# w1 of a decode MLP in one load of 28 KB to a partition, and the last rows of wo in the small slot

## The chip, the cores and the metric

The kernel runs on one core of a Trainium2 chip. The metric is device time in microseconds (us): 392.85 us for the kernel before, the median of 3 runs (392.83 to 392.96). All arithmetic is float32.

## The reference

One decode step (one token for each of B = 8 sequences) through an attention block over a sliding window of a cache and an MLP with a squared relu, both with adaptive layer norm. What is computed:

```python
W = min(4096, max(256, Sk // 4))                      # 2048 of 8192 cached positions
mod = (silu(c) @ w_mod).reshape(8, 6, 1, -1)          # sa, ca, ga, sb, cb, gb
h = layernorm(x) * (1 + ca) + sa
q = (h @ wq)                                          # 32 query heads, 8 kv heads, head size 128
scores = einsum("bhqd,bhkd->bhqk", q, k[:, :, Sk - W:]) * 128 ** -0.5
o = einsum("bhqk,bhkd->bhqd", softmax(scores), v[:, :, Sk - W:])
x = x + ga * (o.reshape(8, 1, 4096) @ wo)             # wo: 4096 x 512
h = layernorm(x) * (1 + cb) + sb
r = relu(h @ w1 + b1)                                 # w1: 512 x 1792
x = x + gb * ((r * r) @ w2 + b2)                      # w2: 1792 x 512
```

## The kernel before, in words

The keys and values of the window are 8 x 8 x 2048 x 128 numbers each and dominate what is read. For each of the 8 kv heads the kernel loads K in two pieces (4 sequences each) and V in two pieces, 4 MB to a piece: K 0 to K 15 and V 0 to V 15. A piece fills 32 KB of each of the 128 partitions.

SBUF has four **big slots** of 32 KB to a partition (one tile, `home`) and one **small slot** of 16 KB (tile `small`). Every large operand passes through one of them. The list `loads` (L186 to L193) names the loads in the order in which they are issued; `pump` (L196) issues from its head as long as the slot size that the next load needs has a free slot, and `done(key)` (L201), called where the last reader of an operand is written in the program, gives a slot back and pumps again. All these loads are issued by SyncE (SP) on one queue, except two gathers of wo rows by GpSimd. Each transfer signals one of eight completion semaphores, DMAHW0 to DMAHW7, which are used in turn: a load also waits until the transfer that used its semaphore before has landed.

The main loop (L586) runs over 38 steps. VectorE transposes K (L234), TensorE makes the scores (L405), a softmax follows (`soft_a` to `soft_g`), and five steps behind the scores come the products with V (L491, `weighted`). For each pair of heads `project_o(j)` (L538) multiplies the attention output with 1024 rows of wo (L544). Of the four pieces of wo rows, j = 0, 1, 2 pass through the small slot under the keys ("wo", j); the last one, j = 3, comes under the key ("tail", 0).

What comes at the end of the program:

- ("tail", 0) is a big slot that holds two things: the last wo rows in its first 16 KB and the first half of w1 (14 KB to a partition) behind them. Two loads fill it (L148 and L136).
- ("w1", 0) is the second half of w1, 14 KB to a partition, in the small slot (L136).
- ("w2", 0) is w2, 28 KB to a partition, in a big slot. It comes in four loads (L136) of 8, 4, 1 and 1 of its 14 row blocks.
- ACT issues five very small loads of b1 and b2 (L580).

After the last `project_o` the tail of the program is one chain. wo's result is added to x (L655, L656), the mean is taken over partitions with a matmul (L660), the normalized rows are turned (L241), and TensorE multiplies them with w1 (L688): for each of 4 row blocks kc, 4 matmuls, each of which is listed as two instructions. Between kc = 1 and kc = 2 stands the matmul of the variance (L683). `w1t[kc // 2]` says that kc = 0, 1 read the tail slot and kc = 2, 3 the small slot. Then b2 enters (L703), VectorE forms the squared relu (L241, L698 to L700), and TensorE multiplies with w2 (L707): 14 blocks f of 4 matmuls. `spin(n)` (L640, L643) puts n matmuls on the identity, whose result nobody reads, at three places of this tail. L715, L716 and a 64 KB store end the program.

Of the kernel before, what the change touches and what calls it, by code (L numbers as in the profile page):

```python
# [20 lines left out]
def tile_adaln_cached_attention_mlp(  # L21
# [16 lines left out]
    B, HKV, SK, DH = k_cache.shape  # L38
    D = wq.shape[0]
# [3 lines left out]
    F = w1.shape[1]  # L43
    NJ = 4 * W // P
    NQ = D // P
    FG = F // NQ
# [58 lines left out]
    big = NJ * DH  # L105
# [7 lines left out]
    held = {}  # L113

    def size_of(key):
        return "small" if key[0] in ("wo", "w1", "far") or key == ("mod", 1) else "big"

    def load(key):
        kind, i = key
        held[key] = free[size_of(key)].pop(0)  # L120
        if key == ("wq", 0):
            return
        t = slots[size_of(key)][held[key]]
        if kind in "KV":

            hk, c = divmod(i, 2)
            v = k_cache[4 * c : 4 * c + 4, hk] if kind == "K" else v_cache[c::2, hk]
            v = v[:, SK - W :, :].rearrange("u (p j) d -> p u (j d)", j=NJ)
            cuts = (0, big // 2, big) if key == ("V", 2 * HKV - 1) else (0, big)
            for x, y in zip(cuts, cuts[1:]):  # L130
                nc.sync.dma_start(t[:, x:y], v[..., x:y])
            return

        def rows(o, v):
            n = v.shape[1] * v.shape[2]
            nc.sync.dma_start(t[:, o : o + n].rearrange("p (a n) -> p a n", n=v.shape[2]), v)  # L136

        w1v = w1.rearrange("(p kc) n -> p kc n", p=P)

        def wo_rows(j):  # L140

            r = 2 * REP * DH
            if j < 2:
                v = wo[j * r : (j + 1) * r].rearrange("(b s) n -> b s n", s=32)[:, :28].rearrange("b (g i) n -> b g (i n)", i=7)
                nc.sync.dma_start(t[:, : 7 * D], v)
                return
            v = wo[j * r : (j + 1) * r, :].rearrange("(p i) n -> p (i n)", p=P)
            nc.sync.dma_start(t[:, : big // 2], v)  # L148

        if kind == "wo":  # L150
            wo_rows(i)
        elif kind == "far":

            nc.gpsimd.memset(t[:, : 4 * D], 0.0)  # L154
            nc.gpsimd.indirect_dma_start(
                out=t[:, : 4 * D],
                out_offset=None,
                in_=wo.rearrange("(a r) n -> a (r n)", r=4),
                in_offset=bass.IndirectOffsetOnAxis(ap=pieces[:, i : i + 1], axis=0),
                bounds_check=wo.shape[0] // 4 - 1,  # L160
                oob_is_err=False,
            )
        elif kind == "mod":

            v = w_mod.rearrange("(p kc) n -> p (kc n)", p=P)
            nc.sync.dma_start(t, v[:, big:] if i else v[:, :big])
        elif kind == "wq":

            o = base[held["wq", 0]]
            nc.sync.dma_start(home[:, o : o + 2 * big], wq.rearrange("(p k) n -> p (k n)", p=P))  # L170
        elif kind == "tail":
            wo_rows(HKV // 2 - 1)
            rows(big // 2, w1v[:, 0:2])
        elif kind == "w1":
            rows(0, w1v[:, 2:4])
        else:
            v = w2.rearrange("(p c) n -> p c n", p=P)
            for lo, hi in ((0, 8), (8, 12), (12, 13), (13, 14)):
                rows(D * lo, v[:, lo:hi])

    def slot(key, n, o=0):

        t = slots[size_of(key)][held[key]][:, o:]
        return t[:, : t.shape[1] // n * n].rearrange("p (a n) -> p a n", n=n)

    loads = [("mod", 0), ("mod", 1), ("wq", 0), ("wq", 1), ("K", 0), ("K", 1)]  # L186
    for n in range(2, 2 * HKV):
# [2 lines left out]
        if n in (4, 11, 14):  # L190
            loads.append(("wo", (4, 11, 14).index(n)))
        loads += [("K", n), ("V", n - 2)]
    loads += [("V", 2 * HKV - 2), ("V", 2 * HKV - 1), ("tail", 0), ("w1", 0), ("w2", 0)]  # L193
    at = [0]

    def pump():  # L196
        while at[0] < len(loads) and free[size_of(loads[at[0]])]:
            load(loads[at[0]])
            at[0] += 1

    def done(*keys):  # L201
        for k in keys:
            free[size_of(k)].append(held.pop(k))
        pump()
# [112 lines left out]
    for i, last in enumerate((16, 8)):  # L317
        at_ = 0
        while at_ < last:
            kc, m = divmod(16 * i + at_, 6)  # L320
# [25 lines left out]
    for kc in range(NQ):  # L346
        w = slot(("wq", kc // 2), 512)[:, kc % 2 * 8 : kc % 2 * 8 + 8]
# [190 lines left out]
    def project_o(j):  # L538

        last = j == HKV // 2 - 1  # L540
        key = ("tail", 0) if last else ("wo", j)
        w = slot(key, D)
        for i in range(8 if j > 1 else 7):
            nc.tensor.matmul(  # L544
                wo_ps[32 * (i % 4) : 32 * (i % 4) + 32, :],
                oT[:, i, :],
                w[:, i, :],
                start=(j == 0 and i < 4),
                stop=(last and i >= 4),
            )  # L550
        if j < 2:

            px = ps_m.tile([P, 512], F32, name="m_ps", tag="m_ps")
            for r in range(4):
                nc.tensor.matmul(px[:, 32 * r : 32 * r + 32], fsel[:, r], oT[:, 7, :], start=True, stop=True)
            px = px[:, :P].rearrange("p (r b) -> p r b", b=32)
            nc.scalar.copy(oX[:, :4], px)
        if not last:
            done(key)

    def far_rows(j):

# [23 lines left out]
    for s in range(N + PV_LAG + 1):  # L586
        g, i = divmod(s, C)
# [16 lines left out]
        if v > C and v % (2 * C) == 1 and v < N:  # L604
            project_o(v // C // 2 - 1)
# [26 lines left out]
        if ends:  # L632
            gather(v // C - 1)

    project_o(HKV // 2 - 1)


# [33 lines left out]
    ssb = work.tile([P, B], F32, name="ssb")  # L671
    nc.vector.tensor_scalar(ssb, sel[:, :B], ssq, None, op0=ALU.mult)

    w1t = [slot(("tail", 0), F, big // 2), slot(("w1", 0), F)]
    w2t = slot(("w2", 0), D)
    ph = ps_m.tile([P, 512], F32, name="m_ps", tag="m_ps")
    nc.tensor.matmul(ph[:, :FG], bsel.rearrange("p g b -> p (g b)"), b1_in, start=True, stop=False)
# [1 line left out]
    for kc in range(NQ):  # L679
        if kc == 2:  # L680

            pb = ps_m.tile([P, 512], F32, name="m_ps", tag="m_ps")
            nc.tensor.matmul(pb[:, :B], ones, ssb, start=True, stop=True)  # L683
            rstd = work.tile([P, B], F32, name="rstd_b")
            nc.scalar.activation(rstd, pb[:, :B], AF.Sqrt, bias=eps, scale=1.0 / D)
            nc.vector.reciprocal(rstd, rstd)
        for g in range(NQ):
            nc.tensor.matmul(  # L688
                ph[32 * g : 32 * g + 32, :FG],
                h2T[:, kc, :],  # L690
                w1t[kc // 2][:, kc % 2, g * FG : (g + 1) * FG],
                start=False,
                stop=(kc == NQ - 1),
            )
# [59 lines left out]
```

## Time and profile before

| what | value |
|---|---|
| timed runs, median of 3 | 392.85 us (392.83 to 392.96) |
| span of the profiled execution, first to last instruction | 390.9 us |
| timed median less that span | 1.95 us |
| PE busy | 260.2 us, 67% |
| DVE busy | 224.2 us, 57% |
| ACT busy | 46.7 us, 12% |
| DMA | 165.04 MB in 7157 packets, mean 422 GB/s |
| SyncE's queue (q1) | 164.17 MB in 6768 packets |

The span is what the profile sees of one execution; the timed runs hold what lies before the first and behind the last instruction as well. All times inside the program are in us from the start of the span. An engine's busy share is an average over the whole span; where it waits, and for what, is read from the chain of waits and from the timeline. PE is TensorE, DVE VectorE, ACT ScalarE, SPq the queue of SyncE.

### The profile page before, as it was taken

How to read it: one execution, taken by the hardware profiler on the slowest of the kernel's cores; microseconds unless marked ns; L12 is line 12 of the kernel's file. 1: busy time of each engine (PE TensorE's matmuls, PEld its weight loads, DVE VectorE, ACT ScalarE, POOL GpSimd, SP SyncE). 2: the span in 40 equal slices, each digit the busy share in tenths (PEclk: the TensorE clock that was granted, in tenths of full speed). 3: DMA queues.
4: the chain of work that ended last, by engine and by line, in shares of the span. 5: the costliest groups of instructions: out<-in, count | busy, mean ns of one | idle time of the engine just before them, and what ended most of it. 6: DMA issues, size and time to landing. Idle time of an engine off the chain costs nothing.

```text
span 390.9 us, 4829 instructions
## 1 busy us (share of the span) xinstructions
PE 260.2 (67%) x2066; PEld 81.8 (21%) x2066; DVE 224.2 (57%) x316; ACT 46.7 (12%) x91; POOL 10.2 (3%) x36
## 2 busy tenths in 40 slices
PE   0080958868337973798379737783788237996895
PEld 0030211112011321242113212321222011322433
DVE  1360099879057935775579457391789057855231
ACT  0120011221003100310031003100201003004010
POOL 4000000000000000030000000200000000000000
PEclk9997789999859996999599969989799859998999
DMA  8999999999999999999999999999999999999995
GB/s 330 431 436 423 434 443 436 438 426 403 441 429 429 431 433 433 431 438 419 431 424 433 431 443 423 428 433 428 433 428 419 443 436 428 425 433 420 416 433 224
DMA packets 7157, 165.04 MB, mean 422 GB/s; under 512 B 1016, under 2 KB 1184, under 8 KB 1440
## 3 DMA queue, kind: packets, MB, share of 16 engines
q1 hardware_dynamic: 6768, 164.17, 98.1%
q0 software_dynamic: 288, 0.53, 0.4%
q8 instruction: 16, 0.26, 0.3%
q10 hardware_dynamic: 80, 0.04, 0.0%
q14 instruction: 5, 0.04, 0.0%
HBM read 166.24 MB, written 0.07 MB: 425 GB/s over the span
## 4 chain that ended last, share of the span: by engine, by line
DMA 53%; DVE 23%; PE 18%; issue 5%; ACT 1%; SPq 0%; ACTq 0%; DVEq 0%
DMA home<-in_A_k_cache_dram 37%; DVE kT L234 12%; DMA home<-in_A_wq_dram 9%; PE s_ps L405 6%; DMA home<-in_B_w_dram 5%; DVE pT L471 5%; PE p_ps L436 3%; PE o_ps L491 3%; PE m_ps L350 2%; DVE pr L464 2%; DMA pr<-in_B_b_dram 2%; DVE mx L419 1%; PE m_ps L421 1%; DVE qbd L368 1%; PE m_ps L441 1%
## 5 line engine op out<-in xcount | busy, mean ns | idle before, releaser
L234 DVE STREAM_TRANSPOSE kT<-home 128x1024 f32<-128x1024 f32 x128 | 151.4, 1220 | 79.7 <-DMA home<-in_A_k_cache_dram 75.8
L405 PE MATMUL s_ps<-kT,qst 128*32 128x512 f32 x512 | 129.0, 1075 | 12.2 <-DVE kT L234 11.9
L491 PE MATMUL o_ps<-home,pT 128*32 128x256 f32 x1024 | 68.5, 390 | 10.8 <-DVE pT L471 10.5
L491 PEld LDWEIGHTS o_ps<-home,pT 128*32 128x32 f32 x1024 | 33.2, 115 | 101.1 <-issue 57.8
L421 PE MATMUL m_ps<-ident,mx 128*1 128x128 f32 x16 | 4.3, 364 | 63.8 <-DVE mx L419 63.8
L405 PEld LDWEIGHTS s_ps<-kT,qst 128*32 128x32 f32 x512 | 14.1, 114 | 30.5 <-DVE kT L234 22.4
L471 DVE STREAM_TRANSPOSE pT<-pr 128x2048 f32<-128x2048 f32 x8 | 18.3, 2281 | 1.0 <-ACT pr L454 1.0
L454 ACT ACTIVATE pr<-pr,own 128x512 f32<-128x512 f32 x16 | 17.8, 1225 | 0.3
L448 ACT ACTIVATE pr<-p_ps,nm 128x512 f32<-128x512 f32 x8 | 5.5, 688 | 102.7 <-DVE nm L445 102.7
L350 PE MATMUL m_ps<-home,oX 128*32 128x512 f32 x64 | 9.5, 757 | 9.8 <-DMA home<-in_A_wq_dram 9.8
L415 ACT COPY ss<-s_ps 128x512 f32<-128x512 f32 x8 | 4.7, 586 | 90.5 <-issue 62.4
L421 PEld LDWEIGHTS m_ps<-ident,mx 128*1 128x1 f32 x16 | 0.7, 81 | 69.0 <-DVE mx L419 69.0
L393 ACT COPY qst<-q_ps 32x128 f32<-32x128 f32 x32 | 8.2, 257 | 52.2 <-PE q_ps L382 52.0
L368 DVE COPY qbd<-m_ps 32x128 f32<-32x128 f32 x8 | 3.0, 373 | 18.8 <-PE m_ps L365 18.7
L436 PE MATMUL p_ps<-ss,perm 128*128 128x512 f32 x16 | 12.9, 896 | 0.0
L445 DVE TENSOR_SCALAR nm<-m_ps 128x1 f32<-128x1 f32 x8 | 1.3, 159 | 17.5 <-PE m_ps L441 17.5
L268 PE MATMUL m_ps<-xsum,sel 128*128 128x1 f32 x2 | 0.6, 363 | 15.5 <-DVE xsum L266 15.5
L526 PE MATMUL m_ps<-o_sb,pick 128*64 128x224 f32 (+2 forms) x48 | 9.9, 345 | 0.9 <-DVE o_sb L509 0.9
L154 POOL MEMSET small<- 128x2048 f32 x2 | 3.6, 1802 | 240.8 <-PE wo_ps L544 240.8
L464 DVE TENSOR_SCALAR pr<-pr,own 128x512 f32<-128x512 f32 x16 | 9.2, 661 | 0.8 <-ACT pr L448 0.8
L528 DVE STREAM_TRANSPOSE tr<-m_ps 64x512 f32<-64x512 f32 x8 | 5.7, 714 | 5.5 <-PE m_ps L526 5.2
L508 DVE TENSOR_SCALAR o_sb<-o_ps,bit 128x128 f32<-128x128 f32 x16 | 5.3, 329 | 4.7 <-PE o_ps L491 4.5
(139 smaller groups left out, 137.7 us busy)
## 6 DMA issues: line engine op xcount, KB each, us to landing
home<-in_A_k_cache_dram SPq DMA_DIRECT2D x16, 4096.0 KB, 31.1
home<-in_A_v_cache_dram SPq DMA_DIRECT2D x15, 4096.0 KB, 20.6
home<-in_w_mod_dram SPq DMA_DIRECT2D x1, 4096.0 KB, 12.7
home<-in_A_v_cache_dram SPq DMA_DIRECT2D x2, 2048.0 KB, 19.5
small<-in_A_wo_dram SPq DMA_DIRECT2D x2, 1792.0 KB
small<-in_w_mod_dram SPq DMA_DIRECT2D x1, 2048.0 KB
small<-in_A_wo_dram SPq DMA_DIRECT2D x1, 2048.0 KB
home<-in_A_wo_dram SPq DMA_DIRECT2D x1, 2048.0 KB, 14.6
```

The lines of the kernel that those rows point to most:

```text
L234: nc.vector.transpose(KTS[q, j][:, rows], k[:, rows, 32 * j : 32 * j + 32])
L350: nc.tensor.matmul(pqs[r][32 * g : 32 * g + 32, :], hT[:, kc, :], w[:, 4 * r + g, :], start=(kc == 0), stop=(kc == NQ - 1),)
L368: nc.vector.tensor_copy(qbd[b, 4 * r : 4 * r + 4, j].rearrange("p g (b t) -> p t g b", t=REP), pT_[b].rearrange("p (t g b) -> p t g b", t= ...
L393: nc.scalar.copy(own[b, :, :, i, 0], pq[b, :P].rearrange("p (c m t) -> p c m t", c=2, t=REP))
L405: nc.tensor.matmul(s_ps[0][32 * g : 32 * g + 32, :], qst[hk % 2][:, P * (4 * c + u) + 32 * j :][:, :32], kT[:, u], start=(c == 0 and j == ...
L421: nc.tensor.matmul(MX_[hk][0:1, :P], mx, ident, start=True, stop=True)
L436: nc.tensor.matmul(sp, perm, SS_.pop(hk), start=True, stop=True)
L454: nc.scalar.mul(X_[hk][..., w], pr, own[:, w : w + 1])
L464: nc.vector.tensor_scalar(X_[hk][..., w], pr, own[:, w : w + 1], None, op0=ALU.mult)
L471: nc.vector.transpose(PT_[hk].rearrange("p e j r -> p j e r"), X_.pop(hk).rearrange("p j x w -> p j (x w)"))
L491: nc.tensor.matmul(O_[n][32 * g : 32 * g + 32, : 2 * DH], PT_[hk][:, e, j : j + 2].rearrange("p j r -> p (j r)"), vt[:, j : j + 2, :].rear ...
L526: nc.tensor.matmul(dest, pick[:, x].rearrange("p t u -> p (t u)"), src, start=True, stop=True)
```

## The change

w1 becomes one operand of 28 KB to a partition that takes a big slot and comes in one load. The last wo rows become ("wo", 3) and take the small slot, as the three pieces of wo rows before them. The key "tail" goes away. Nothing of the computation changes.

```diff
     def size_of(key):
-        return "small" if key[0] in ("wo", "w1", "far") or key == ("mod", 1) else "big"
+        return "small" if key[0] in ("wo", "far") or key == ("mod", 1) else "big"
...
-        elif kind == "tail":
-            wo_rows(HKV // 2 - 1)
-            rows(big // 2, w1v[:, 0:2])
         elif kind == "w1":
-            rows(0, w1v[:, 2:4])
+            rows(0, w1v)
...
-    loads += [("V", 2 * HKV - 2), ("V", 2 * HKV - 1), ("tail", 0), ("w1", 0), ("w2", 0)]
+    loads += [("V", 2 * HKV - 2), ("V", 2 * HKV - 1), ("wo", 3), ("w1", 0), ("w2", 0)]
...
     def project_o(j):
 
         last = j == HKV // 2 - 1
-        key = ("tail", 0) if last else ("wo", j)
-        w = slot(key, D)
+        w = slot(("wo", j), D)
...
         if not last:
-            done(key)
+            done(("wo", j))
...
-    w1t = [slot(("tail", 0), F, big // 2), slot(("w1", 0), F)]
+    w1t = slot(("w1", 0), F)
...
-                w1t[kc // 2][:, kc % 2, g * FG : (g + 1) * FG],
+                w1t[:, kc, g * FG : (g + 1) * FG],
```

The lines behind L171 move up by three or four: L544 becomes L540, L643 L639, L683 L679, L688 L684, L703 L699 and L707 L703.

On SyncE, at the end of its list, the loads behind the last V. `in_A_wo_dram` is wo and `in_B_w_dram` is w1 (3584 or 7168 elements to a partition) or w2 (4096, 2048, 512, 512); in brackets stand the semaphores that the load waits for.

```order
-L148 DMA home<-in_A_wo_dram 128x4096 [waits DMAHW6_49,DMAHW0_49,DVE_49]
-L136 DMA home<-in_B_w_dram 128x3584 [waits DMAHW1_49,DVE_49]
-L136 DMA small<-in_B_w_dram 128x3584 [waits DMAHW3_49,DMAHW2_49]
-L136 DMA home<-in_B_w_dram 128x4096 [waits DMAHW3_49,PE_49]
-L136 DMA home<-in_B_w_dram 128x2048 [waits DMAHW4_49,PE_49]
+L148 DMA small<-in_A_wo_dram 128x4096 [waits DMAHW3_49,DMAHW0_49]
+L136 DMA home<-in_B_w_dram 128x7168 [waits DMAHW6_49,DMAHW1_49,DVE_49]
+L136 DMA home<-in_B_w_dram 128x4096 [waits DMAHW2_49,PE_49]
+L136 DMA home<-in_B_w_dram 128x2048 [waits DMAHW3_49,PE_49]
+L136 DMA home<-in_B_w_dram 128x512 [waits DMAHW4_49,PE_49]
 L136 DMA home<-in_B_w_dram 128x512 [waits DMAHW5_49,PE_49]
-L136 DMA home<-in_B_w_dram 128x512 [waits DMAHW6_49,PE_49]
```

The wo load now waits for the small slot's last load (DMAHW3) and no longer for K 15 (DMAHW6) and VectorE; the two w1 loads have become one, and each piece of w2 has moved to the semaphore before.

On TensorE, the products with w1 in the tail of the program. `pr_1684` is the buffer that holds the turned normalized rows (its number is 1683 in the changed kernel). Before:

```order
L688 MATMUL m_ps<-home,pr_1684 32x448 [waits DMAHW1_49,DVE_49]
L688 MATMUL m_ps<-home,pr_1684 32x448 x7
L683 MATMUL m_ps<-ssb,ones 128x8 [waits DVE_49]
L688 MATMUL m_ps<-small,pr_1684 32x448 [waits DMAHW2_49]
L688 MATMUL m_ps<-small,pr_1684 32x448 x7
```

And with the change:

```order
L684 MATMUL m_ps<-home,pr_1683 32x448 [waits DMAHW6_49,DMAHW1_49,DVE_49]
L684 MATMUL m_ps<-home,pr_1683 32x448 x7
L679 MATMUL m_ps<-ssb,ones 128x8 [waits DVE_49]
L684 MATMUL m_ps<-home,pr_1683 32x448 x8
```

The order of the instructions is the same. The wait on a w1 load in the middle is gone, and the wait at the head is for the load of all of w1.

## Rows read from the trace of the kernel before

**Rows 1.** The page: the chain that ended last, share of the span by engine.

```profile
DMA 53%; DVE 23%; PE 18%; issue 5%; ACT 1%; SPq 0%; ACTq 0%; DVEq 0%
```

**Rows 2.** The chain of waits, 350 to 391: start us, us, what.

```profile
364.63 21.30 DMA home<-in_B_w_dram
...
385.97 1.30 PE m_ps L707 x40
...
387.27 0.47 PE m_ps L707 x8
```

**Rows 3.** Windows: us, busy of PE, PEld, DVE, ACT, POOL, granted clock, DMA share, GB/s.

```profile
310.00:340.00 30.00, 18.45 (x132) 5.24 (x136) 19.57 (x24) 3.00 (x4) 0.00 (x0) 0.78 1.00 431
...
350.00:360.00 10.00, 6.43 (x58) 2.92 (x59) 5.31 (x9) 4.47 (x6) 0.47 (x1) 0.88 0.95 403
...
370.00:380.00 10.00, 9.12 (x66) 3.02 (x66) 2.99 (x13) 1.13 (x4) 0.00 (x0) 1.00 1.01 428
380.00:386.00 6.00, 4.71 (x82) 2.71 (x75) 1.48 (x4) 0.00 (x0) 0.00 (x0) 1.00 0.97 398
```

**Rows 4.** Timeline of TensorE from 370: start, us, instructions [idle before <-releaser].

```profile
370.34 1.92 PE L544 MATMUL wo_ps<-home,oT 128*32 128x512 f32 x16 [1.07 <-DVE oT L532]
...
375.67 1.13 PE L643 MATMUL q_ps<-ident 128*128 128x512 f32 x2
376.73 1.71 PE L688 MATMUL m_ps<-home,pr 128*32 128x448 f32 x16
378.37 0.39 PE L683 MATMUL m_ps<-ssb,ones 128*128 128x8 f32 x2
378.69 1.71 PE L688 MATMUL m_ps<-small,pr 128*32 128x448 f32 x16
...
380.74 1.98 PE L643 MATMUL q_ps<-ident 128*128 128x512 f32 x4
383.58 1.96 PE L707 MATMUL m_ps<-home,pr 128*32 128x128 f32 x64 [0.85 <-DMA home<-in_B_w_dram]
385.97 1.73 PE L707 MATMUL m_ps<-home,pr 128*32 128x128 f32 x48 [0.44 <-DMA home<-in_B_w_dram]
```

**Rows 5.** Waits of SyncE's queue: us in total, times, longest us.

```profile
SPq L148 <- DMA home<-in_A_v_cache_dram: 9.1, 1, 9.1
...
SPq L136 <- DMA home<-in_A_v_cache_dram: 4.5, 1, 4.5
SPq L136 <- DMA pr<-in_B_b_dram: 4.3, 5, 1.6
```

**Rows 6.** Timeline of SyncE's queue, the loads behind the last V.

```profile
355.35 0.33 SPq L148 DMA_DIRECT2D home<-in_A_wo_dram  x1
360.24 0.33 SPq L136 DMA_DIRECT2D home<-in_B_w_dram  x1
362.28 0.33 SPq L136 DMA_DIRECT2D small<-in_B_w_dram  x1
363.31 3.52 SPq L136 DMA_DIRECT2D home<-in_B_w_dram  x4
```

**Rows 7.** DMA queue q1 in 310 to 340, then 384 to 387: packets, MB, share.

```profile
q1 hardware_dynamic: 441, 12.88, 100.0%
...
q1 hardware_dynamic: 348, 0.94, 79.6%
```

**Rows 8.** Timeline of TensorE at three earlier waits.

```profile
80.96 0.25 PE L477 MATMUL m_ps<-zs,tsel 128*64 128x8 f32 x2 [1.81 <-DVE zs L466]
...
332.02 1.07 PE L491 MATMUL o_ps<-home,pT 128*32 128x256 f32 x16 [1.08 <-DVE pT L471]
...
357.43 1.86 PE L491 MATMUL o_ps<-home,pT 128*32 128x256 f32 x16 [2.95 <-DVE pT L471]
```

**Rows 9.** Two more windows, columns as in rows 3.

```profile
77.00:82.00 5.00, 3.19 (x16) 0.66 (x20) 4.72 (x8) 2.96 (x4) 0.00 (x0) 1.00 0.98 416
...
357.00:361.00 4.00, 3.57 (x20) 1.35 (x20) 1.29 (x4) 0.00 (x0) 0.47 (x1) 0.57 1.04 435
```

## The prediction

> **What bounds the kernel now.** I read the chain of waits first. It is more than half DMA [rows 1], and its last links are a w2 load issued at 364.63, then 40 matmuls of L707 from 385.97 and the last 8 from 387.27 [rows 2]. So the end of the program is set by when the last bytes of w2 land, plus half a microsecond of matmuls and a short rest. The next view asks whether the DMA engines could have brought them sooner. The windows show the 16 engines busy all the way: shares of 1.00 from 310 to 340 and 1.01 from 370 to 380, 0.95 and 0.97 in the two weakest stretches [rows 3]. (A share can pass 1, since a packet counts where it starts.) A queue that is never empty for long ends when its bytes are through, whenever its loads are issued. Last I read TensorE's timeline from 370 on [rows 4]: what stands there between the first product with w1 and the last with w2 is the only thing near the DMA in length, and the change works on it.
>
> **The change, step by step.** The bytes and their order in the queue stay: last wo rows, w1, w2.
>
> *The wo rows.* They go to the small slot and no longer wait for K 15 and for VectorE's transposes of it. Their issue does not move for that. It stood for 9.1 us until a V load had landed [rows 5], and of the waits in the change's order of SyncE the one that this was, DMAHW0 (the semaphore that V 14 used before), is still there; wo 2, whose slot they take, has its last reader in step 30 of the loop, a step before this load is issued. So I expect the issue at 355.35 as before [rows 6]. If it were 9.1 us earlier, nothing would be won, because both halves of V 15 stand ahead of it in full queues. Its reader L544 waited 1.07 us for VectorE's oT and not for the load [rows 4]. Cost: 0, covered by the queue.
>
> *w1 and w2 at issue.* The w1 load waits for DMAHW1 (first half of V 15, landed at 360.24 in the old run) and is issued where the first half of w1 was. One semaphore less is used, so each w2 piece takes the one that its forerunner had: the first piece is due at 362.28, where w1's second half was issued, instead of 363.31 [rows 6]. The waits on the b1 and b2 loads, 4.3 us in five of them [rows 5], become four. All that is SyncE's time ahead of a full queue: worth 0, and if the queue did run dry there, about 1 us of it.
>
> *The packets.* w1 was 2 x 128 packets of 14 KB, 16 to an engine; it becomes 128 of 28 KB, 8 to an engine (one packet to a partition: the 29 KB that a packet has on average in 310 to 340 are the 32 KB rows of K and V with a few short closing writes [rows 7]). What a packet costs beside its bytes comes from two stretches of the DMA view [rows 7]. In 310 to 340, 441 packets with 12.88 MB took 480 engine-us (16 x 30 x 1.000); in 384 to 387, 348 packets with 0.94 MB took 38.2 (16 x 3 x 0.796). Two equations with a cost per packet f and per MB r give r = 36.9 us and f = 0.010 us. Eight data packets and one closing write less on each engine are **0.09 us** off the end of w2: 387.27 becomes 387.18. Packets of 32 KB, longer than the new ones, are what the first stretch is made of, so I expect no penalty for length.
>
> *When w1 can be read.* This is the cost. Before, L688 read the first half of w1 from 376.73 while the second was landing, and the second from 378.69 without a wait [rows 4]. Now the first of the 32 instructions needs the whole. When had the whole landed? At 378.69 at the latest. From the other side: the first wait on w2 ended at 383.55 (383.58 for the matmul) and the next at 385.97; the 1 MB between took 2.42 us, so the 2 MB before 383.55 took 4.84, which puts w1's end at 378.71. I take 378.69, less the 0.09 for packets: 378.60. TensorE, free at about 376.8, thus gets a **new wait of 1.8 us**, and L684 (the old L688) starts 1.87 later than the old 376.73. Everything behind it on TensorE and VectorE moves by that: the sum over squares, b2, the filling matmuls, the squared relu.
>
> *What takes the delay up.* In the old run the products with w2 did not start when TensorE was free. The filling matmuls of L643 began at 380.74, are listed until 382.72, and L707 came at 383.58 after 0.85 us for the first piece of w2; it lost 0.44 before the second, and stood 0.27 before 387.27 [rows 2, 4]. From the start of L688 to the earliest start of L707 were 5.92 us (382.72 less 0.07, by which neighbouring rows overlap: L683 starts at 378.37 where L688's 16 end at 378.44). So L703 (the old L707) can start at 378.60 + 5.92 = 384.52. By then the first piece is there (383.46), the second comes at 385.88 for matmuls that would start at about 386.2, and the third and fourth about when they are wanted. Without waits the 112 instructions take 1.96 + 1.73 - 0.27 - 0.27 (the tail counted twice, one matmul) = 3.15, ending at **387.67**. The DMA's own bound is 387.18 + 0.47 = **387.65**. Before it was 387.27 + 0.47 = 387.74.
>
> *Sum.* Less 0.07 us by these values. The bounds: -0.09, if only the DMA counts; +0.3, if the 0.07 and the tails do not overlap (378.60 + 5.99 + 1.96 + 1.46 = 388.01). Nearer is the lower end, since the overlap is in the rows at every seam. The profiled execution spans 390.9 us; the timed median of 392.85 is 1.95 us more, outside the first and last instruction, and nothing of the change lies there. I predict **392.8 us**, no difference that can be told: a measurement of this kernel tells about 0.2%, 0.8 us.
>
> **The rivals.**
>
> *Slower: TensorE's clock falls in the new wait.* After 2.95 us without a matmul, 16 instructions of L491 took 1.86 us from 357.43 where the same 16 took 1.07 at 332.02, and the granted clock of 357 to 361 was 0.57, which is 3.4 us at the lower of its two levels (1.2 GHz instead of 2.4) [rows 8, 9]. The new wait is 1.8 us in the middle of the end's chain, where only that chain counts. For it speaks that the stretch before is thin as well; against it that 1.81 us idle before 80.96 left the clock at 1.00 in 77 to 82 [rows 8, 9], and that L643's filler stands right before and the dense L684 right behind. If it falls, 3.4 us at half speed lose 1.7 us of work: L703 starts at 386.2 and ends at 389.4, **394.5 us**. The point from which it decides is a wait between 1.81 and 2.95. The Trainium skill (TensorE: Matmul & The Clock Gate, Part 1) gives these two clocks and lets an idle array fall to the lower; the 0.57 agrees, and the 1.00 shows that not every wait does it. Chance 0.12.
>
> *Faster: a load less saves the fixed time of a load.* That would be the case if between two loads the engines stood still. L136's issues would then show up as dips, but the share of 370 to 380, where both halves of w1 and the start of w2 were carried, is 1.01 [rows 3]. If there were such a dip of 2 us at the seam, w1 would be whole at 376.7, L684 would start where L688 did, and the path 376.73 + 5.92 + 3.15 ends at 385.8: **390.9 us**. The Trainium skill (DMA: Bandwidth & Descriptors, Anatomy of one DMA) fits 2.0 us of fixed time for each DMA on the gpsimd path, most of it the receipt of the last write; by it the sum would be that 390.9. The trace differs: a share of 1.01 leaves no room for such a stop between two queued loads. Chance 0.03.
>
> *The change does nothing at this place:* w1 lands whole well before TensorE wants it, as it would if the second half had been there at 376.7. Then only the 0.09 is left, 392.76. It speaks against it that 2 MB of w2 cannot have taken 6.8 us. It falls within the same 0.2%; chance 0.05.
>
> **How the numbers follow.** My forecast has 0.80, the rivals 0.12, 0.03 and 0.05. Within 0.2%: 0.84 (the forecast less a tail of 0.01, and the third rival). Slower by over 0.2%: 0.12. Faster: 0.03 and 0.01 of the forecast's tail. The forecast and the third rival alone hold more than 8 in 10, with -0.1 to +0.3 us about 392.85. The low end, 392.4, takes in half of what the shares of 0.95 over 10 us and 0.97 over 6 us leave open (0.68 us), if the new order of issue should fill it. The high end, 393.7, takes in a clock that falls for half as long as the row shows (0.85 us). A full fall and the 2 us gain stay outside.
>
> **What would show it.** In the profile of the changed kernel: the wo load still issued near 355, w1 near 360, w2's first piece near 362; L684 starting near 378.6 after a wait on a w1 load of 1.8 us; L703 near 384.5 with little or no wait on w2; the last matmuls ending at 387.6 to 388.0; a granted clock of 1.00 from 376 on. I am wrong if L684 starts before 377.5 or after 379.3, if the clock is below 1.00 between 378 and 388, or if the DMA share in 360 to 386 leaves 0.95 to 1.05.

## The result and the profile after

The changed kernel takes **394.34 us** (median of 12 runs, 392.95 to 395.82), the kernel before 392.79 (12 runs, 392.66 to 393.15). The ratio is 1.0040, with a 95% interval of 1.0027 to 1.0053: slower by 1.6 us, outside the range that was predicted. Together with the second series below there are 24 timed runs of the changed kernel, and they lie in three groups with gaps between them: 8 at 392.73 to 393.18, 10 at 394.20 to 394.65, 6 at 395.58 to 395.82. The kernel before has one group, 0.5 us wide.

The profiled execution took 394.25 us, with a span of 392.5, so it is one of the middle group. First the page's chain by engine:

```profile
DMA 46%; PE 24%; DVE 23%; issue 5%; ACT 1%; SPq 0%; DVEq 0%; ACTq 0%
```

Beside [rows 1] the DMA's share has fallen from 53 to 46% and TensorE's has risen from 18 to 24%: the chain that ends last no longer ends in a w2 load but in TensorE's products. Out of its rows (start us, us, what):

```profile
376.75 1.80 issue
378.55 3.21 PE m_ps L684 x16
...
386.05 3.24 PE m_ps L703 x112
```

The DMA itself is as busy as before. Windows, columns as in rows 3:

```profile
350.00:360.00 10.00, 6.43 (x59) 2.90 (x60) 5.32 (x9) 4.46 (x6) 0.47 (x1) 0.89 0.95 405
360.00:370.00 10.00, 8.35 (x119) 3.95 (x117) 3.05 (x7) 0.00 (x0) 0.00 (x0) 0.94 1.03 434
370.00:380.00 10.00, 7.36 (x40) 2.34 (x44) 2.76 (x11) 0.87 (x3) 0.00 (x0) 0.91 0.98 421
380.00:386.00 6.00, 6.00 (x39) 1.93 (x31) 1.68 (x5) 0.27 (x1) 0.00 (x0) 0.86 0.96 399
```

Shares of 0.95 to 1.03; the three of these windows that [rows 3] has were at 0.95 to 1.01. What differs stands in the column ahead of the share: TensorE's granted clock was 1.00 from 370 to 386 before, and is 0.91 and 0.86 now. Its timeline, the rows that answer to [rows 4]:

```profile
370.29 1.92 PE L540 MATMUL wo_ps<-small,oT 128*32 128x512 f32 x16 [1.07 <-DVE oT L529]
...
375.63 1.12 PE L639 MATMUL q_ps<-ident 128*128 128x512 f32 x2
378.55 3.21 PE L684 MATMUL m_ps<-home,pr 128*32 128x448 f32 x16 [1.80 <-issue]
381.69 0.39 PE L679 MATMUL m_ps<-ssb,ones 128*128 128x8 f32 x2
382.01 1.71 PE L684 MATMUL m_ps<-home,pr 128*32 128x448 f32 x16
...
384.07 1.98 PE L639 MATMUL q_ps<-ident 128*128 128x512 f32 x4
385.98 3.26 PE L703 MATMUL m_ps<-home,pr 128*32 128x128 f32 x112
```

The new wait is there, 1.80 us before the first product with w1. (The view names "issue" as its releaser, since it found no load behind it; in the run late_half below, where the wait is about as long, it names the w1 load.) The first 16 instructions of L684 then take 3.21 us, where the next 16, the same products on the same tile, take 1.71. The clock in the windows behind the wait says why:

```profile
376.00:378.00 2.00, 0.75 (x2) 0.00 (x0) 0.00 (x0) 0.00 (x0) 0.00 (x0) 1.00 0.85 363
378.00:380.00 2.00, 1.45 (x8) 0.45 (x12) 0.00 (x0) 0.00 (x0) 0.00 (x0) 0.56 0.96 410
380.00:382.00 2.00, 2.00 (x14) 0.52 (x6) 0.00 (x0) 0.00 (x0) 0.00 (x0) 0.58 0.98 418
382.00:384.00 2.00, 2.00 (x19) 0.71 (x18) 0.41 (x2) 0.27 (x1) 0.00 (x0) 1.00 0.97 405
```

At 1.00 until 378, 0.56 and 0.58 to 382, 1.00 again from there. What is missing, 0.44 and 0.42 of 2 us, is 1.72 us, which makes some 3.4 us at 1.2 GHz instead of 2.4. The products with w2 start at 385.98 instead of 383.58, and now without a wait for w2.

SyncE did what was expected. The rows that answer to [rows 6], and below them to [rows 5]:

```profile
355.29 0.33 SPq L148 DMA_DIRECT2D small<-in_A_wo_dram  x1
360.24 5.90 SPq L136 DMA_DIRECT2D home<-in_B_w_dram  x5
```

```profile
SPq L148 <- DMA home<-in_A_v_cache_dram: 9.0, 1, 9.0
...
SPq L136 <- DMA home<-in_A_v_cache_dram: 4.6, 1, 4.6
SPq L136 <- DMA pr<-in_B_b_dram: 3.6, 4, 1.9
```

### The profile page after: what moved, and what is told of

The parts are those of the page before. It is cut to its first block, busy times and chain, and to the rows that moved or that the text cites. A ratio compares the mean times of both kernels' runs of the same rounds, so it can differ in the third digit from the quotient of the medians.

```text
span 392.5 us, 4827 instructions
## 1 busy us (share of the span) xinstructions
PE 259.5 (66%) x2066; PEld 81.4 (21%) x2066; DVE 224.1 (57%) x316; ACT 46.8 (12%) x91; POOL 10.2 (3%) x36
## 2 busy tenths in 40 slices
DMA packets 7013, 165.04 MB, mean 421 GB/s; under 512 B 1000, under 2 KB 1168, under 8 KB 1424
## 4 chain that ended last, share of the span: by engine, by line
DMA 46%; PE 24%; DVE 23%; issue 5%; ACT 1%; SPq 0%; DVEq 0%; ACTq 0%
DMA home<-in_A_k_cache_dram 37%; DVE kT L231 12%; DMA home<-in_A_wq_dram 9%; PE s_ps L402 6%; PE o_ps L488 5%; DVE pT L468 5%; PE p_ps L433 3%; PE m_ps L347 2%; DVE pr L461 2%; DVE mx L416 1%; PE m_ps L684 1%; PE q_ps L639 1%; PE m_ps L523 1%; PE wo_ps L540 1%; PE m_ps L703 1%
## 5 line engine op out<-in xcount | busy, mean ns | idle before, releaser
L488 PE MATMUL o_ps<-home,pT 128*32 128x256 f32 x1024 | 68.6, 391 | 10.8 <-DVE pT L468 10.5
L488 PEld LDWEIGHTS o_ps<-home,pT 128*32 128x32 f32 x1024 | 32.8, 115 | 101.2 <-issue 58.4
L540 PE MATMUL wo_ps<-small,oT 128*32 128x512 f32 x60 | 7.7, 597 | 1.1 <-DVE oT L529 1.1
```

The costliest lines, as they stand in the source:

```text
L488: nc.tensor.matmul(O_[n][32 * g : 32 * g + 32, : 2 * DH], PT_[hk][:, e, j : j + 2].rearrange("p j r -> p (j r)"), vt[:, j : j + 2, :].rear ...
L540: nc.tensor.matmul(wo_ps[32 * (i % 4) : 32 * (i % 4) + 32, :], oT[:, i, :], w[:, i, :], start=(j == 0 and i < 4), stop=(last and i >= 4),)
```

## The experiments

Three theories stood against each other. The **clock theory**: the new wait lets TensorE's granted clock fall, and that is the loss. The **start theory**: the products with w1 start 1.9 us later, and that is the loss, whatever the clock does. The **load theory**: the one large load or the small slot for the wo rows brings w2 later.

**fill3: fill the wait.** Three filling products instead of one ahead of L684, so that the products with w1 start as late as in the changed kernel while TensorE has no wait.

```diff
     nc.tensor.matmul(ph[:, :FG], bsel.rearrange("p g b -> p (g b)"), b1_in, start=True, stop=False)
-    spin(1)
+    spin(3)
```

> The changed kernel with three filling products instead of one between b1 and the first product with w1, so that TensorE is busy until about 378.3. Clock theory (the wait of 1.8 us lets the granted clock fall, and that costs 1.5 us): clock 1.00 from 376 to 388, the wait before the first product with w1 under 0.4 us, the time 392.7 to 393.0 us in every run, with a spread like that of the kernel before (0.5 us). Start theory (the later start of the products with w1 is what costs, the clock only shows beside it): the start is as late as in the changed kernel, so the time stays near 394.3. Load theory (the one load or the small slot brings w2 later): also near 394.3, with the last w2 piece landing 1 us or more after 387.3.

Measured: 392.95 us (11 runs, 392.76 to 393.64) against 392.77 before, ratio 1.0007 (0.9998 to 1.0016). Its timeline from the filler on:

```profile
376.12 2.84 PE L639 MATMUL q_ps<-ident 128*128 128x512 f32 x6
378.90 1.71 PE L684 MATMUL m_ps<-home,pr 128*32 128x448 f32 x16
380.54 0.39 PE L679 MATMUL m_ps<-ssb,ones 128*128 128x8 f32 x2
```

L684 starts 0.35 us later than in the changed kernel and takes 1.71 instead of 3.21; the clock is 1.00 in every window from 376 to 388. So the start theory falls: the start is late and the time is that of the kernel before, within what can be told. The load theory falls too, since loads and slots are those of the changed kernel. One thing missed its expectation: 3 of the 11 runs are at 393.55 to 393.64. This profile is of a run at 393.09; what the three did is open. An estimate: in look7 below, TensorE comes free at 378.03 only, and two more filling products (2.84 less 1.12, 1.72 us) would start L684 near 379.7, 0.8 us behind this profile. That would be about 393.9, so the three may be runs with a late chain; no profile shows it.

**two_loads: undo the one load, keep the slots.** w1 in its big slot, wo 3 in the small one, but w1 in two loads of 14 KB.

```diff
         elif kind == "w1":
-            rows(0, w1v)
+            rows(0, w1v[:, 0:2])
+            rows(2 * F, w1v[:, 2:4])
```

> The changed kernel, slots as there, but w1 comes in two loads of 14 KB to a partition into its big slot, and the first half of the products waits for the first load only. Clock and start theories: the wait of 1.8 us is gone, the first product with w1 starts near 376.7 as in the kernel before, 392.8 us in every run. Load theory, if the small slot for the last wo rows is the cause: near 394.3. If the one load is the cause: 392.8.

Measured: 392.80 us (11 runs, 392.67 to 393.13), ratio 1.0000 (0.9991 to 1.0009), L685 from 376.67. The small slot for the wo rows costs nothing. All of the loss needs the one load, by the wait that it makes.

**late_half: the wait without the load.** The kernel before with all its loads and slots; only the row blocks of w1 are taken in another order, so that the half that lands last is wanted first.

```diff
-    for kc in range(NQ):
-        if kc == 2:
+    for n, kc in enumerate((2, 3, 0, 1)):
+        if n == 2:
...
-                stop=(kc == NQ - 1),
+                stop=(n == NQ - 1),
```

> The kernel before, its loads and slots untouched, with the four row blocks of w1 taken in the order 2, 3, 0, 1, so that the first product waits for the half that lands last. Clock theory: a wait of about 1.8 us before the first product with w1, the clock down to 0.5 to 0.6 behind it in most runs, and times spread like those of the changed kernel: some near 393.0, most near 394.3, median 394.0 to 394.7. Start theory: near 394.3 in every run, with a narrow spread. Load theory: 392.8, since the loads are those of the kernel before.

Measured: 12 runs, 6 at 392.88 to 393.12, 4 at 394.29 to 394.56, 2 at 395.77 and 395.87. The median of 393.71 lies in the gap between two groups; the ratio is 1.0028 (1.0012 to 1.0045). The profile is of a run at 394.29:

```profile
375.69 1.12 PE L643 MATMUL q_ps<-ident 128*128 128x512 f32 x2
378.71 3.16 PE L688 MATMUL m_ps<-small,pr 128*32 128x448 f32 x16 [1.90 <-DMA small<-in_B_w_dram]
381.80 0.39 PE L683 MATMUL m_ps<-ssb,ones 128*128 128x8 f32 x2
382.12 1.71 PE L688 MATMUL m_ps<-home,pr 128*32 128x448 f32 x16
```

The same three groups, the same wait and the same slow 16 instructions, with the old loads. The median came out lower than expected, because half of the runs were in the group near 393.0 and not a third. The row has a number besides: the first product that waits for the last part of w1 starts at 378.71, where the prediction had taken 378.69 for the landing.

**nofill: a longer wait.** The changed kernel without the filler ahead of L684.

```diff
-    spin(1)
     for kc in range(NQ):
```

> The changed kernel without the filling product between b1 and the first product with w1, so that TensorE stands from about 375.7 to 378.55, 2.9 us instead of 1.8. Clock theory: 2.9 us is as long as the wait before 357.43, after which the clock was low in every profile so far. Hardly any run stays near 393, where the changed kernel has 8 of 24; median 394.3 or more. If what counts is only that the products with w1 start late: as the changed kernel, the same groups in the same shares.

Measured: 6 runs, 392.82 and five at 394.31 to 394.67, median 394.46, ratio 1.0035 (1.0022 to 1.0048). The wait before the first product is 2.89 us and the clock 0.70, 0.50 and 0.95 in the three windows of 2 us from 378. The wait is longer only at its front, since the products with w1 start at 378.71, when w1 is there; and what is missing in these windows (0.60, 1.00 and 0.10 us) is again about 3.4 us at half the clock. So the longer wait costs no more here. Whether it makes a fall more frequent can't be told: five of six runs fell by their times, against 16 of 24 of the changed kernel. The one run at 392.82 was not profiled.

**fill2: half of the added filler.** `spin(2)` where fill3 has `spin(3)`.

> The changed kernel with two filling products instead of one before the products with w1: the wait is halved, to about 0.9 us where the chain comes on time, and TensorE is free before w1 has landed. Clock theory: a wait of 0.9 us is shorter than those that left the clock alone (1.07 before the product with wo in every profile), so clock 1.00 from 376 to 388 and one group of runs at 392.75 to 393.1, a little under the run with three filling products since the filler ends before w1 is there. If any wait at this place lowers the clock: a group near 394.3.

Measured: 392.90 us (11 runs, 392.82 to 393.13) against 392.84, ratio 1.0002 (0.9993 to 1.0011). One group, none of the late runs of fill3. In the profiled run the chain came late, for a reason that follows below, and the filler already closed the wait; no profile shows the wait of 0.9 us that was expected.

**b2_early: work instead of filler.** The product that brings in b2 goes ahead of the products with w1, into a buffer of its own (`ps_o`), with `spin(2)` behind it.

```diff
+    py = ps_o.tile([P, 512], F32, name="o_ps")
+    nc.tensor.matmul(py[:, :P], qsel.rearrange("p q b -> p (q b)"), b2_in, start=True, stop=False)
-    spin(1)
+    spin(2)
...
-    py = ps_m.tile([P, 512], F32, name="m_ps", tag="m_ps")
-    nc.tensor.matmul(py[:, :P], qsel.rearrange("p q b -> p (q b)"), b2_in, start=True, stop=False)
```

> The changed kernel with the product that brings in b2 put ahead of the products with w1, into the wait, and two filling products behind it: the wait shrinks from 1.8 to about 0.5 us, and the part of the chain between w1 and w2 is 0.4 us shorter than in the run with three filling products. Clock theory: clock 1.00 from 376 to 388, one group of runs. Then the chain ends before the DMA's bound again, so that the 0.09 us of the fewer packets could show: 392.65 to 392.8, against 392.95 with three filling products and 392.77 for the kernel before. Start theory: near 394.0.

Measured: 392.94 us (11 runs, 392.67 to 393.05) against 392.82, ratio 1.0002 (0.9993 to 1.0010). One group, as expected, but not below the kernel before, so the 0.09 us of the packets stays unseen. No version here beats the kernel before.

**The changed kernel again, ten times.** after_again is a second series of 12 runs; look1 to look9 are one profiled run each. None has an edit.

> The changed kernel again, beside the others on one chip. Clock theory: times in groups, near 393.0 where the clock holds, near 394.3 where it falls for one stretch, and the group that this profile's run falls into is told by its clock between 376 and 388: 1.00 with 393.0, about 3.4 us at half with 394.3. Start and load theories: one narrow group near 394.3, whatever the clock.

> The changed kernel once more, for a profile of the slowest group of its runs (near 395.7) if it comes. Clock theory: 393.0 goes with clock 1.00 from 376 to 388, 394.3 with about 3.4 us at half there, 395.7 with about twice as much at half.

> The same as the look before: 393.0 with clock 1.00 from 376 to 388, 394.3 with about 3.4 us at half, 395.7 with about twice as much.

> The changed kernel, for a profile of the group near 395.7. Clock theory: 395.7 goes with about 6.8 us at half clock behind the wait before w1, 394.3 with 3.4, 393.0 with none and a wait under 1 us, since the clock's earlier fall behind 357 lasted longer and the chain comes 1 us later.

> The same as the look before: 395.7 with about 6.8 us at half clock behind the wait before w1, 394.3 with 3.4, 393.0 with none and a wait under 1 us.

> The same as the two looks before: 395.7 with about 6.8 us at half clock behind the wait before w1, 394.3 with 3.4, 393.0 with none and a wait under 1 us.

> Of a run near 395.7: clock theory, about 6.8 us at half behind the wait before w1, the first product with w2 near 387.4 instead of 386.0. If it is something else: 3.4 us at half as near 394.4, and 1.3 us lost at another place, in the DMA or before 370.

> As look6: near 395.7 about 6.8 us at half and the first product with w2 near 387.4 by the clock theory, otherwise the loss at another place.

> As look6: near 395.7 about 6.8 us at half and the first product with w2 near 387.4 by the clock theory, otherwise the loss at another place.

> As look6: near 395.7 about 6.8 us at half and the first product with w2 near 387.4 by the clock theory, otherwise the loss at another place.

The series gave 5 runs at 392.73 to 393.05, 4 at 394.39 to 394.65, 3 at 395.58 to 395.76. With the profile after, there are eleven profiles of the changed kernel, and they sort without an exception:

| time, us | profiles | wait before L684, us | clock behind it | clock in 361 to 365 |
|---|---|---|---|---|
| 392.74 to 393.02 | 6 | 0.52 to 0.80 | 1.00 | 0.67 to 0.75 |
| 394.25 to 394.52 | 4 | 1.45 to 1.80 | low for about 3.4 us | 0.87 to 0.99 |
| 395.60 | 1 | 2.02 | low for about 6.8 us | 1.00 |

The last is look6, the only profile of its group. TensorE's timeline, then the windows:

```profile
378.67 3.22 PE L684 MATMUL m_ps<-home,pr 128*32 128x448 f32 x16 [2.02 <-issue]
381.81 0.60 PE L679 MATMUL m_ps<-ssb,ones 128*128 128x8 f32 x2
382.34 2.74 PE L684 MATMUL m_ps<-home,pr 128*32 128x448 f32 x16
...
387.34 3.26 PE L703 MATMUL m_ps<-home,pr 128*32 128x128 f32 x112
```

```profile
376.00:378.00 2.00, 0.65 (x2) 0.00 (x0) 0.00 (x0) 0.00 (x0) 0.00 (x0) 0.91 0.81 346
378.00:380.00 2.00, 1.33 (x8) 0.46 (x12) 0.00 (x0) 0.00 (x0) 0.00 (x0) 0.50 1.00 426
380.00:382.00 2.00, 2.00 (x13) 0.41 (x6) 0.00 (x0) 0.00 (x0) 0.00 (x0) 0.50 0.92 393
382.00:384.00 2.00, 2.00 (x14) 0.88 (x18) 0.20 (x1) 0.27 (x1) 0.00 (x0) 0.50 1.00 417
384.00:386.00 2.00, 2.00 (x16) 0.67 (x9) 0.81 (x2) 0.00 (x0) 0.00 (x0) 0.88 0.93 371
```

Both halves of L684 are slow, and L703 starts at 387.34, where 387.4 was expected. So in this run of the third group the fall is the same, and lasts twice as long.

The table's last column shows the fall behind the wait of 2.95 us in [rows 8], 20 us earlier: where that fall lasted longer, the clock in 361 to 365 is lower and the chain comes later. In look7, of the group near 393:

```profile
357.44 1.94 PE L488 MATMUL o_ps<-home,pT 128*32 128x256 f32 x16 [2.95 <-DVE pT L468]
...
361.20 7.35 PE L488 MATMUL o_ps<-home,pT 128*32 128x256 f32 x112
...
371.57 1.92 PE L540 MATMUL wo_ps<-small,oT 128*32 128x512 f32 x16 [1.07 <-DVE oT L529]
...
378.55 1.71 PE L684 MATMUL m_ps<-home,pr 128*32 128x448 f32 x16 [0.52 <-issue]
```

The same instructions of L488 in the profile after, of the group near 394.3:

```profile
360.92 6.35 PE L488 MATMUL o_ps<-home,pT 128*32 128x256 f32 x112
```

So they take 7.35 us in look7 instead of 6.35, L540 starts at 371.57 instead of 370.29, and TensorE has 0.52 us to wait for w1 instead of 1.80. The clock then holds, and the run ends sooner by 1.5 us. In these eleven profiles, the runs whose chain comes late to the wait end first.

That the short wait is what holds the clock is not shown by the table, since the groups differ long before it. Near 81 us stands the wait for zs of [rows 8], 1.80 to 1.82 us long in all eleven. The windows behind it, first in the profile after, then in look7:

```profile
81.00:85.00 4.00, 2.92 (x22) 0.74 (x26) 4.00 (x4) 0.00 (x0) 0.00 (x0) 0.57 0.91 393
81.00:85.00 4.00, 2.79 (x28) 0.58 (x24) 3.75 (x4) 0.00 (x0) 0.00 (x0) 1.00 0.93 401
```

The clock fell here in the four profiles near 394.3 (0.57 to 0.64) and in none of the other seven. In 90 to 94 it fell in the six near 393 (0.57 or 0.58), behind a wait of 1.89 to 2.37 us, and in none of the other five, where that wait was 0.80 to 1.68 us. So a run's clock tells its group 300 us before w1 is wanted. What the experiments show is that with the wait filled (fill3, fill2, b2_early) none of 33 runs is near 394.3 or above.

## Why the prediction was wrong

**What held.** The wo load was issued at 355.29 and waited 9.0 us for the same V load; w1 was issued at 360.24, and the waits on b1 and b2 went from five to four. The DMA stayed full. The new wait was predicted as 1.8 us and measured as 1.80, the start of L684 as 378.60 and measured as 378.55. The sum itself, 392.8, with bounds of 392.76 to 393.15 from -0.09 and +0.3, is where the clock holds: the first group's 392.73 to 393.18, and fill2's 392.90. That agreement is in part luck: the sum has a wait of 1.8 us with a clock of 1.00 behind it, and none of the eleven profiles has the two together. In the first group the wait was 0.52 to 0.80 us, because TensorE came free at about 378.0 (look7) and not at 376.8; the time agrees since the sum used only the start of L684 and the clock.

**What failed.** The sum lets TensorE run on at 1.00 behind the new wait, and the step "How the numbers follow" gives the first rival, that the clock falls there, a chance of 0.12. The prediction's own sign of being wrong, a clock below 1.00 between 378 and 388, is what came. The rival's mechanism, place and price were right: 3.4 us at half clock, 394.5 us, against a median of 394.34 and 394.20 to 394.65 for its group; the loss on L684 was 1.50 us (3.21 less 1.71) where it had 1.7. It was held for unlikely on the ground that "1.81 us idle before 80.96 left the clock at 1.00", and the point of decision was put "between 1.81 and 2.95". One profiled run of another place in the program was read as a limit. The runs show that it is none. In the eleven profiles the clock at L684 held with waits up to 0.80 us and fell with 1.45 and more. And at the very place from which the limit was read, it fell in the run late_half. Its timeline, then two windows, and the second window in the kernel before:

```profile
80.90 0.25 PE L477 MATMUL m_ps<-zs,tsel 128*64 128x8 f32 x2 [1.81 <-DVE zs L466]
```

```profile
77.00:81.00 4.00, 2.19 (x12) 0.37 (x11) 3.79 (x7) 2.96 (x4) 0.00 (x0) 1.00 0.96 406
81.00:85.00 4.00, 2.92 (x22) 0.74 (x26) 4.00 (x4) 0.00 (x0) 0.00 (x0) 0.57 0.95 410
```

```profile
81.00:85.00 4.00, 2.92 (x26) 0.70 (x26) 4.00 (x4) 0.00 (x0) 0.00 (x0) 1.00 0.93 401
```

The same wait of 1.81 us that left 1.00 in the kernel before is followed by 0.57 here. In the 18 profiles of all kernels this wait is 1.80 to 1.82 us long, and the clock fell behind it in six (0.57 to 0.64 in 81 to 85) and held in twelve. So the right chance was to be taken from many waits in many runs; from one, it was nearly open. At L684, 16 of the 24 timed runs fell, by the groups that their times are in.

**What was missed in the price.** A fall twice as long, 395.6 us, was not among the cases; a quarter of the runs have it, and it lies 1.9 us above the range's high end of 393.7.

**The other rivals.** A load less saves no fixed time of 2 us: the first product that waits for the end of w1 starts at 378.71 with two loads (late_half) and at 378.55 to 378.83 with one (the eleven profiles). That w1 would be there before it is wanted is refuted by the wait. The 0.09 us for fewer packets could not be told: the packets fell to 7013 from 7157, which are the 128 of w1 and the 16 closing writes, but no comparison resolves so little.

## What to carry to other kernels

Merging two loads can cost nothing on a full DMA queue and still be slow, because a matmul engine that could start on the first half now stands. Count such a new wait of a microsecond or two as a possible fall of the clock, at about 1.5 us for each 3.4 us at half speed on the end's chain, and keep the load split or fill the wait; both give the old time back here. Where the times of a kernel lie in groups, take profiles until each group has one, and do not take a limit from one wait in one profile.

## What the runs showed of the hardware that was not expected

The same wait of 1.81 us at the same instruction left the granted clock at 1.00 in one execution and took it to 0.57 in another. At the wait before L684 the low stretch lasted about 3.4 us in four profiles and 6.8 in one. A wait of 2.89 us (nofill) gave about the 3.4 us again. What decides between them is open; the length of the wait alone does not. A run's clock at 81 to 94 us already goes with the group that its time will be in, in all eleven profiles of the changed kernel.
